# Attention's products in two 64-row groups on two banks, with a merged Gram product and a re-ordered list of work

## The chip, the cores and the metric

The kernel runs on one core of a Trainium2 chip. The metric is device time in microseconds (us), the median of three runs of one kernel: 1371.57 us for the kernel before, its runs from 1369.68 to 1371.94.

## What is computed

The reference is an attention over 32 pooled queries, a mixture of eight experts, and a gated product, one after the other. Batch, heads, sequence and head size are 8, 8, 576 and 64, so there are 4608 tokens of width 512.

```python
def _attn_ref(q, k, v, p):                      # p: 32 pooled queries per head
    p_packed = sm_attn(p, k, v)                 # softmax(p k^T / 8) v, 32 x 64 per head
    return sm_attn(q, p_packed, p_packed)       # softmax(q pp^T / 8) pp
def _moe_ref(x, expert_emb, tau, w1, w2):       # D=512, E=8, F=1024
    logits = xn @ en.T / tau                    # both normalised; one expert per token
    ...
        h = np.maximum(x[mask] @ w1[e], 0.0)
        out[mask] = gate_w[mask, None] * (h @ w2[e])
def _moe2_ref(x, w_a, w_b, w_out):              # d_ff = 1536
    return (x @ w_a * (x @ w_b)) @ w_out
```

## The kernel before

The kernel runs three stages, one after the other on TensorE: attention, experts (class `Moe`), gated product (class `Moe2`). A planner (`Sched`) decides the order of the work when the program is built. Each step is an `op` with the engines it may use, an assumed duration on each, the ops it depends on, a priority (lower goes first) and the buffers it takes and frees. `run` repeatedly takes, among the steps that could start earliest by the assumed durations, the one of lowest priority, and emits its instructions. Each engine, and the SP queue with its DMAs, then runs its own list strictly in that order.

**Attention, per batch.** `prep` loads p, k and v, transposes p and k on TensorE (`pT_mm`, `kT_mm`), and multiplies the pooled queries with the keys (`s1_mm`, lines 302 and 307). Heads come in pairs: a 128-row transposed tile holds two tokens' 64 rows, an even one above an odd one. `s1_mm` reads all 128 rows, with weights that are zero in the half not wanted (p is laid between zero columns in `pz`, and transposed in two positions `a`). So each group `g` of heads takes two products `a`, each into one bank of PSUM, with four heads in four 32-column groups of the array. `s1_ev` copies the scores to SBUF, `mx` and `exp` make the softmax there. `eT_mm` transposes the exponentials, and `pp_mm` (line 373) multiplies them with v: its two groups `g` lie in rows 0 to 63 and 64 to 127, in two banks. `ppT_mm` turns the result, `gr_mm` (lines 412, 413) makes for each head the 32 x 32 Gram matrix of the pooled values and its products with the eight expert embeddings, and `gr_ev` spreads the former into a block-diagonal matrix of 128 columns by multiplying with `blk`.

`query` loads and transposes q, and `rest` works in `NW` = 3 units of three token groups per batch. One unit is `s2_mm` (scores against the pooled keys, line 496, weights of 64 columns), `mx`, `sub`, `exp`, `total`, `norm`, a transpose `aT_mm`, and `x_mm` (line 539), which multiplies the attention weights with the 128 + 8 columns of the block-diagonal Gram matrix and the expert products, one product per token group and `g`, over all 128 rows. `dots`, `sq` and `add` make from it the eight dot products and the squared norm of each token in `c.nd`.

**PSUM** has eight banks. Attention uses three tags: `tr` (four banks: all transposes, `s1`, `gr`, and what the expert stage does ahead), `sm` (two: `s2` and `pp`) and `x` (two: `x_mm`).

**Experts.** `experts` chooses the expert for one batch of nine token groups: a product with `c.pair` (line 691), some 14 short steps on VectorE (recorded on line 672), one power on GpSimd (line 701). Batches 0 to 6 are done within attention and batch 7 at the start of the expert stage. `Moe.fetch` loads the weights of that expert, `zed` (line 961) multiplies the pooled keys with its first weights (512 columns at a time, four heads in four column groups, all 128 rows with zero halves, for each `g` into its own bank), and `up_mm` and `down_mm` follow. Batch 0's loads and its `zed` lie within attention, the other seven within the expert stage. `pT_dram` keeps the transposed pooled keys with their zero halves, 128 KB for each `g`.

Of the kernel before, what the change touches and what calls it, by code (L numbers as in the profile page):

```python
# [22 lines left out]
NI = NT // 64  # L23
AHEAD = 0.65
QA = 1.5
# [9 lines left out]
def make_consts(nc, c, keep, pool, emb, tau, psum, en, esq):  # L35
# [7 lines left out]
    c.blk = pool.tile([128, 4, NP], F32, name="blk")  # L43
    nc.gpsimd.memset(c.blk, 0.0)
    for j in range(4):
        nc.gpsimd.memset(c.blk[32 * j:32 * j + 32, j, :], 1.0)
# [25 lines left out]
class Sched:  # L72
# [4 lines left out]
    EPS, LAT, SAME = 0.05, 0.2, 0.06  # L77

# [11 lines left out]
    def op(self, engs, fn, deps=(), prio=0.0, take=(), free=(), lat=None, bias={}, start=0.0, after=None,  # L90
           behind=(), land=0.0):
# [6 lines left out]
        o.behind, o.land = behind, land  # L98
# [5 lines left out]
    def run(self, most=None, **clock):  # L104


        todo = list(self.ops)
        while todo:
            cand = []
            for n, o in enumerate(todo[:most]):  # L110
# [14 lines left out]
                for e, dur in o.engs.items():  # L125
                    at = max([clock.get(e, 0.0), ready.get(None, 0.0)]
                             + [d.end + (self.SAME if d.eng == e and d.lat <= self.LAT else d.lat) for d in o.deps])
                    key = at + dur + o.bias.get(e, 0.0)
                    if best is None or key < best[0]:
                        best = (key, at, dur, e)  # L130
# [6 lines left out]
            o.eng, o.end = e, at + dur  # L137
            if e != "none":
                clock[e] = o.end
# [10 lines left out]
NW = CI // 3  # L150


def attention(ctx, tc, c, q, k, v, p, a_dram, pT_dram, consts, more):
    nc = tc.nc
    W = 4 * NP + E
# [3 lines left out]
    for name, pools in dict(io="kvq", kt=["pT", "kt"] + [f"kT{m}" for m in range(4)], q=["qT"], e=["e", "eT"],  # L159
# [5 lines left out]
    ps_pool = dict(tr=c.ps_tr, sm=c.ps_sm, x=c.ps_x)  # L165
    pzs = [sb["pT"].tile([128, 2, 3 * D], F32, name=f"pz{i}") for i in range(2)]
    for t in pzs:
        nc.vector.memset(t, 0.0)
# [7 lines left out]
    own["a"] = [sb["a"].tile([128, 12, NP + 1], F32, name=f"as{i}") for i in range(sizes["a"])]  # L176
    for g in range(2):
        own[f"ppT{g}"] = [sb["pc"].tile([128, 4, 2, NP], F32, name=f"ppT{g}{i}") for i in range(sizes[f"ppT{g}"])]
# [5 lines left out]
    S_ = Sched(sizes)  # L184
    op, Buf = S_.op, Sched.Buf
# [11 lines left out]
    def psum(n, key):  # L197
        T_[key] = ps_pool[n].tile([128, 512], F32, tag=n, name=n)
        return T_[key]
# [11 lines left out]
    o_en = op({"T": 0.33}, en_mm, take=[t_en], prio=-4.0, start=EN0)  # L211
# [9 lines left out]
    def prep(b):  # L221
# [25 lines left out]
        def pT_mm(e):  # L247
            ps = psum("tr", ("pTp", b))
            tile_("pT", ("pT", b), [128, 2, 2, 128])
            for g in range(2):  # L250
                for a in range(2):
                    nc.tensor.transpose(
                        ps[:, (2 * g + a) * 128:(2 * g + a + 1) * 128], T_["pz", b][:, g, (1 - a) * D:(3 - a) * D],
                        c.ident)

        def pT_ev(e):
            copy(e, T_["pT", b], T_["pTp", b].rearrange("p (g a q) -> p g a q", g=2, a=2))

        t, bpT = Buf("tr"), Buf("pT")
        o = op({"T": 0.44}, pT_mm, deps=[o_p], prio=at(0), take=[t, bpT], free=[bp])  # L260
        o_pT = op({"A": 0.47, "V": 0.6}, pT_ev, deps=[o], prio=at(0), free=[t])
# [19 lines left out]
        for m in (0, 1, 2, 3, 4):  # L281
            t = Buf("tr")
            bkT.append(Buf(f"kT{m}" if m < 4 else "kt"))
            o = op({"T": 0.44}, kT_mm(m), deps=[o_k[m // 2]] if m < 4 else o_k, prio=at(0.05 * m), take=[t, bkT[m]],
# [5 lines left out]
        for g in range(2):  # L290
            def s1_mm(a, g=g):
                def f(e):
                    ps = psum("tr", ("s1p", b, g, a))
                    if (g, a) == (0, 0):
                        tile_("e", ("e", b), [128, CI, 2, D])

                    def w(j):
                        h = 2 * j + g
                        return T_["pT", b][:, h // 4, a, h % 4 * 32:h % 4 * 32 + 32]

                    for j in range(4):
# [3 lines left out]
                    if a == 0:  # L305
                        for j in range(4):
                            nc.tensor.matmul(
                                ps[32 * j:32 * j + 32, 256:320], lhsT=w(j),
                                rhs=T_["kT", b, 4][:, j, 64 * g:64 * g + 64], start=True, stop=True)
                return f  # L310

            def s1_ev(a, g=g):
                def f(e):
                    s = (slice(0, 5), slice(5, 9))[a]
                    n = s.stop - s.start
                    copy(e, T_["e", b][:, s, g], T_["s1p", b, g, a][:, 0:n * D].rearrange("p (i q) -> p i q", i=n))
                return f

            def mx(e, g=g):
                T_["mx", b, g] = m = st.tile([128, 1], F32, tag="mx1", name="mx1")  # L320
                nc.vector.tensor_reduce(out=m, in_=T_["e", b][:, :, g], axis=AX.XY, op=ALU.max)
                nc.vector.tensor_scalar(out=m, in0=m, scalar1=-0.125, scalar2=None, op0=ALU.mult)
# [1543 lines left out]
```

## Time and profile before

| | us |
|---|---|
| median of three runs | 1371.57 |
| the profiled execution, its own time | 1371.34 |
| its span, from the first to the last instruction | 1369.5 |
| TensorE busy | 1335.0 (97%) |
| VectorE busy | 790.8 (58%) |
| ScalarE busy | 591.9 (43%) |
| GpSimd busy | 106.5 (8%) |
| DMA | 278 MB, mean 203 GB/s |

PE is TensorE's products, PEld its loads of weights, DVE is VectorE, ACT ScalarE, POOL GpSimd, SPq the queue of SP, from which nearly all DMAs are issued. Busy time is the union of the durations, and a product's duration includes its way through the array: where products overlap, the time from the start of one group to the start of the next says more of its cost than its duration.

### The profile page before, as it was taken

To read this page: it belongs to the slowest core of one execution; us is meant where nothing else is said; L and a number is where in the kernel's file an instruction comes from. 1 tells how busy PE (TensorE), PEld (TensorE's weight loads), DVE (VectorE), ACT (ScalarE), POOL (GpSimd) and SP (SyncE) were. 2 spreads that over 40 slices of the span, in tenths; PEclk is the share of its full clock that TensorE was granted. 3 is DMA by queue.
4 is the path that set the end of the run, shared out by engine and by line. 5 is a ranking of instruction groups with operands and counts; after the bars stand their busy time and mean duration, and the time that the engine had idled before them with its cause. 6 is when DMAs were issued, how large, how long until landed. Compare 5 with 4: busy or idle time off the path is not lost. (4 is left out here: it accounts for less than half of the span.)

```text
span 1369.5 us, 26692 instructions
## 1 busy us (share of the span) xinstructions
PE 1335.0 (97%) x10263; PEld 1214.9 (89%) x10263; DVE 790.8 (58%) x1635; ACT 591.9 (43%) x1222; POOL 106.5 (8%) x234
## 2 busy tenths in 40 slices
PE   8998989999999999999999999999999999999997
PEld 6767778999999998999899999999999989999996
DVE  5787867666766655798554356434634363444342
ACT  5656524444444434565533244234433442343232
POOL 1121210101001000000100010001000010001001
PEclk9999999999999999999999999999999999999999
DMA  8878366778876735777865576557655665556552
GB/s 286 279 244 258 119 223 228 253 241 262 289 247 200 238 116 187 254 254 268 254 170 162 162 232 176 161 157 221 188 160 160 206 199 159 160 166 198 160 161 65
DMA packets 169272, 278.04 MB, mean 203 GB/s; under 512 B 16937, under 2 KB 68521, under 8 KB 169137
## 3 DMA queue, kind: packets, MB, share of 16 engines
q1 hardware_dynamic: 162704, 257.35, 60.9%
q0 software_dynamic: 6272, 18.88, 4.0%
q8 instruction: 84, 1.38, 0.4%
q14 instruction: 52, 0.42, 0.1%
q10 hardware_dynamic: 160, 0.02, 0.0%
HBM read 219.04 MB, written 57.15 MB: 202 GB/s over the span
## 5 line engine op out<-in xcount | busy, mean ns | idle before, releaser
L1443 DVE TENSOR_TENSOR s<-s,s 128x384 f32<-128x384 f32 x324 | 176.8, 556 | 340.8 <-ACT s L1579 338.4
L765 PE MATMUL pb<-xq,wq 128*128 128x384 f32 x504 | 170.2, 338 | 1.5 <-DVE s L1443 0.7
L765 PE MATMUL pa<-xq,wq 128*128 128x384 f32 x504 | 169.6, 337 | 1.6 <-DVE s L1443 1.6
L1692 PE MATMUL o<-oh,gh 128*128 128x512 f32 x432 | 170.3, 394 | 0.9 <-ACT osb L1712 0.9
L1693 PE MATMUL o<-ol,gh 128*128 128x512 f32 x432 | 170.4, 394 | 0.0
L1694 PE MATMUL o<-oh,gl 128*128 128x512 f32 x432 | 170.4, 394 | 0.0
L767 PE MATMUL pa<-xq,wq 128*128 128x384 f32 x504 | 170.3, 338 | 0.0
L767 PE MATMUL pb<-xq,wq 128*128 128x384 f32 x504 | 170.1, 337 | 0.0
L766 PE MATMUL pb<-xq,wq 128*128 128x384 f32 x504 | 170.0, 337 | 0.0
L766 PE MATMUL pa<-xq,wq 128*128 128x384 f32 x504 | 169.9, 337 | 0.0
L765 PE MATMUL dn<-hh,w2h 128*128 128x288 f32 x512 | 153.0, 299 | 0.0
L1579 ACT COPY s<-pa 128x384 f32<-128x384 f32 x180 | 86.5, 481 | 149.9 <-PE pa L767 149.8
L767 PE MATMUL dn<-hh,w2l 128*128 128x288 f32 x512 | 151.0, 295 | 0.0
L766 PE MATMUL dn<-hl,w2h 128*128 128x288 f32 x512 | 150.3, 294 | 0.0
L1579 ACT COPY s<-pb 128x384 f32<-128x384 f32 x180 | 86.5, 481 | 140.7 <-PE pb L767 140.6
L765 PEld LDWEIGHTS dn<-hh,w2h 128*128 128x128 f32 x512 | 96.1, 188 | 11.7 <-ACT w2h L994 5.9
L765 PEld LDWEIGHTS pb<-xq,wq 128*128 128x128 f32 x504 | 94.7, 188 | 11.8 <-DVE c L1443 1.6
L765 PEld LDWEIGHTS pa<-xq,wq 128*128 128x128 f32 x504 | 94.7, 188 | 10.0 <-DVE s L1443 2.2
L766 PEld LDWEIGHTS pb<-xq,wq 128*128 128x128 f32 x504 | 94.6, 188 | 8.4
L766 PEld LDWEIGHTS pa<-xq,wq 128*128 128x128 f32 x504 | 94.6, 188 | 7.5
L1694 PEld LDWEIGHTS o<-oh,gl 128*128 128x128 f32 x432 | 81.0, 187 | 18.8
L766 PEld LDWEIGHTS dn<-hl,w2h 128*128 128x128 f32 x512 | 96.8, 189 | 0.0
(192 smaller groups left out, 2436.1 us busy)
## 6 DMA issues: line engine op xcount, KB each, us to landing
wq<-ws SPq DMA_DIRECT2D x420, 256.0 KB, 2.8
ws<-wq SPq DMA_DIRECT2D x84, 256.0 KB, 3.7
raw<-in_moe_w_dram SPq DMA_DIRECT2D x36, 512.0 KB, 6.2
rawb<-in_moe_w_dram SPq DMA_DIRECT2D x28, 512.0 KB, 9.1
k<-in_k_dram SPq DMA_DIRECT2D x16, 576.0 KB, 5.4
v<-in_v_dram SPq DMA_DIRECT2D x16, 576.0 KB, 5.5
q<-in_q_dram SPq DMA_DIRECT2D x16, 576.0 KB, 5.1
xr<-x2T SPq DMA_DIRECT2D x20, 384.0 KB, 4.9
```

The lines of the kernel that those rows point to most:

```text
L765: nc.tensor.matmul(ps, lhsT=wh, rhs=xh, start=start, stop=False, **kw)
L766: nc.tensor.matmul(ps, lhsT=wh, rhs=xl, start=False, stop=False, **kw)
L767: nc.tensor.matmul(ps, lhsT=wl, rhs=xh, start=False, stop=stop, **kw)
L1443: VT = lambda out, a, b, o: V.tensor_tensor(out=out, in0=a, in1=b, op=o)
L1579: A.copy(out=T[n, key], in_=ps[n, names_bank[key]])
L1692: nc.tensor.matmul(a, lhsT=gh[:, h, s], rhs=wh, start=first, stop=False)
L1693: nc.tensor.matmul(a, lhsT=gh[:, h, s], rhs=wl, start=False, stop=False)
L1694: nc.tensor.matmul(a, lhsT=gl[:, h, s], rhs=wh, start=False, stop=last)
```

## The change

1. `s1_mm` reads 64 rows instead of 128. The two positions `a` lie in two row groups, each with its own bank, and are one step. p is loaded twice side by side in place of the zeros (two DMAs), and transposed in two blocks instead of four. `mx` and `exp` read the scores from PSUM; the copies `s1_ev` are gone. `mx` has a second reduction, `exp` a second activation.
2. `x_mm` works in two row groups `r` on two banks, with 64 + 8 columns each, so each token group takes four products in place of two. `sq` and `dots` read both banks; dot products come in two parts that are added by `pairs`.
3. `zed` reads 64 rows; both `g` are one step in two banks, in attention too. `pT_dram` keeps 64 KB per batch.
4. `gr_mm` makes one 128-column product over all four heads and keeps the diagonal blocks by `blk`, in place of four of 32 columns.
5. Units of four and five token groups (two per batch) in place of three of three. `s2_mm` pairs two token groups in each product; the last of the five stands alone.
6. PSUM: `tr` keeps four banks; the other four are `two`, two tiles of two banks, for `s1`, `pp`, `s2`, `x` and `zed`.
7. `experts` is called twice, for batches 0 to 3 within attention and for 4 to 7 at the start of the expert stage.
8. The planner gets other durations and adds a priority offset for each kind of step (`SHIFT`), a bias against VectorE where ScalarE can do a step (`VB`), and a least time of 4.3 us for each 127 products (`LF`, `CHUNK`).

```diff
-QA = 1.5
+QA = 2.0
+    VB, SHIFT, CHUNK, LF = 0.0, {}, 127, 0.0
...
+        if self.SHIFT:
+            o.prio += self.SHIFT.get(".".join([x for x in fn.__qualname__.split(".") if x != "<locals>"][-2:]), 0.0)
...
+            if self.LF and e == "T" and o.mm:
+                mm, left, x = o.mm, dur, at
+                while had + mm >= self.CHUNK:
+                    k = self.CHUNK - had
+                    part = left * k / mm
+                    x, left, mm, had = max(x + part, chunk + self.LF), left - part, mm - k, 0
+                    chunk = x
+                had += mm
+                o.end = x + left
...
-NW = CI // 3
+UNITS = ((0, 4), (4, 5))
+NW = len(UNITS)
...
-    sizes = dict(tr=4, sm=2, x=2, k=3, v=3, q=3, qT=4, e=2, eT=2, a=2, an=3, aT=2, sq=2, pz=2, pT=2, kt=1,
+    sizes = dict(tr=4, two=2, k=3, v=3, q=3, qT=6, e=2, eT=2, a=2, an=3, aT=2, sq=2, pz=2, pT=2, kt=1,
...
+    S_.LAT, S_.VB, S_.SHIFT, S_.LF = 0.22, 0.15, SHIFT, 4.3
...
-            turn_ = T_["pz", b] = pzs[b % 2]
-            nc.sync.dma_start(out=turn_[:, :, D:2 * D], in_=p[b].rearrange("(g j) p d -> (j p) g d", j=4))
+            t = tile_("pz", ("pz", b), [128, 2, 2, D])
+            for r in range(2):
+                nc.sync.dma_start(out=t[:, :, r], in_=p[b].rearrange("(g j) p d -> (j p) g d", j=4))
...
+                for j in range(4):
+                    for a in range(2):
                         nc.tensor.matmul(
-                            ps[32 * j:32 * j + 32, 0:256].rearrange("q (i p) -> q i p", i=4), lhsT=w(j),
-                            rhs=T_["kT", b, j][:, :, 64 * g:64 * g + 64], start=True, stop=True)
...
+                            ps[32 * j:32 * j + 32, a, 0:256].rearrange("q (i p) -> q i p", i=4), lhsT=w(j, a),
+                            rhs=T_["kT", b, j][D * a:D * a + D, :, 64 * g:64 * g + 64], start=True, stop=True)
...
+                nc.vector.tensor_reduce(out=m[:, 0:1], in_=ps[:, :, 0:256], axis=AX.XY, op=ALU.max)
+                nc.vector.tensor_reduce(out=m[:, 1:2], in_=ps[:, 0, 256:320], axis=AX.X, op=ALU.max)
...
+                w = T_["ppT", b, g][rows, g]
+                nc.tensor.matmul(ps[:, 0:128], lhsT=w.rearrange("p j k -> p (j k)"),
+                                 rhs=w.rearrange("p j k -> p (j k)"), start=True, stop=True)
                 for j in range(4):
-                    w = T_["ppT", b, g][rows, j, g, :]
-                    nc.tensor.matmul(ps[32 * j:32 * j + 32, 0:NP], lhsT=w, rhs=w, start=True, stop=True)
...
+            for i in range(n):
+                off = 64 * (first + i)
                 for g in range(2):
-                    off = 192 * w + 64 * i
-                    nc.tensor.matmul(ps[64 * g:64 * g + 64, i * W:i * W + W], lhsT=T_["aT", b][:, g, off:off + 64],
-                                     rhs=T_["gr", b, g], start=True, stop=True)
...
+                    for r in range(2):
+                        nc.tensor.matmul(xp()[64 * g:64 * g + 64, r, i],
+                                         lhsT=T_["aT", b][rows2[r], g, off:off + 64],
+                                         rhs=T_["gr", b, g][rows2[r], r], start=True, stop=True)
...
+            def mm(e, f=f, st=st):
+                st["ps"] = psum()
+                for j in range(4):
+                    for g in range(2):
+                        rows = slice(D * g, D * g + D)
+                        nc.tensor.matmul(st["ps"][32 * j:32 * j + 32, g, :], lhsT=self.pr[rows, j, :],
+                                         rhs=self.raw1[j][rows, f], start=True, stop=True)
...
+                e_ops, g_ops = experts(nc, c, tmp, 0, KNOWN, tr)
+                e = chain(S, e_ops, 4.5 * KNOWN + LG, of(0, KNOWN), step=0.05)
...
+                moe.before(S, lambda: c.ps_two.tile([128, 2, 512], F32, tag="two", name="two"), 18.0, e)
```

## Rows read from the trace of the kernel before

**Rows 1.** Busy time of each engine by stage: attention, experts, gated product.

```profile
0.00:182.80 182.80, 163.11 (x3410) 127.41 (x3410) 137.50 (x433) 107.83 (x252) 34.21 (x49) 0.99 0.68 224
182.80:522.80 340.00, 338.08 (x2534) 315.25 (x2533) 216.71 (x352) 143.75 (x235) 30.27 (x40) 0.99 0.71 231
522.80:1369.50 846.70, 833.82 (x4323) 772.20 (x4321) 436.54 (x850) 340.28 (x736) 41.98 (x145) 1.00 0.62 187
```

**Rows 2.** Stretches of attention: PE, PEld, DVE, ACT, POOL, PEclk, DMA share, GB/s.

```profile
0.00:10.00 10.00, 4.75 (x23) 4.36 (x24) 4.53 (x17) 3.46 (x6) 3.73 (x21) 1.00 0.71 240
...
120.00:140.00 20.00, 16.73 (x331) 13.32 (x319) 13.95 (x49) 11.62 (x29) 4.63 (x5) 1.00 0.72 233
140.00:170.00 30.00, 28.68 (x726) 22.70 (x722) 25.03 (x88) 15.04 (x38) 5.12 (x5) 1.00 0.30 100
170.00:182.80 12.80, 7.15 (x78) 5.63 (x77) 9.91 (x35) 5.28 (x11) 1.79 (x1) 0.81 0.07 27
```

**Rows 3.** TensorE's timeline around 77 and 80 us: start, duration, count.

```profile
76.71 0.64 PE L302 MATMUL tr<-kT,pT 128*32 128x256 f32 x8
77.16 0.29 PE L307 MATMUL tr<-kt,pT 128*32 128x64 f32 x8
77.39 0.92 PE L539 MATMUL x<-gr,aT 128*64 128x136 f32 x12
78.23 0.33 PE L398 MATMUL tr<-ident,pc 128*128 128x128 f32 x1
78.49 1.13 PE L496 MATMUL sm<-ppT,qT 128*64 128x64 f32 x32
79.55 0.33 PE L458 MATMUL tr<-ident,q 128*128 128x128 f32 x1
...
80.25 0.27 PE L412 MATMUL tr<-ppT 64*32 64x32 f32 x7
...
80.50 0.64 PE L302 MATMUL tr<-kT,pT 128*32 128x256 f32 x8
81.07 0.33 PE L458 MATMUL tr<-ident,q 128*128 128x128 f32 x1
```

**Rows 4.** TensorE's timeline in the expert stage, around `zed`.

```profile
213.64 1.92 PE L961 MATMUL up<-raw,pr 128*32 128x512 f32 x16
215.49 0.40 PE L765 MATMUL dn<-hh,w2h 128*128 128x288 f32 x1
```

**Rows 5.** TensorE alone, 0.24 us within `pp_mm`: products begun.

```profile
70.78:71.02 0.24, 0.24 (x32) 1.00 0.96 401
```

**Rows 6.** Products of `zed` (line 961) in the expert stage: PE, PEld busy.

```profile
182.80:522.80 340.00, 26.93 (x224) 5.84 (x224) 0.99 0.71 231
```

**Rows 7.** Groups of instructions by line: count, busy us, mean ns, idle before.

```profile
L203 ACT COPY e<-tr 128x320 f32<-128x320 f32 (+1 forms) x28 | 11.1, 399 | 6.1 <-PE tr L307 4.7 <-PE tr L302 0.7
...
L252 PE MATMUL tr<-ident,pz 128*128 128x128 f32 x32 | 5.5, 298 | 4.9 <-POOL en L54 4.5 <-DVE gr L205 0.3
...
L691 PE MATMUL tr<-nd,pair 128*128 128x81 f32 x14 | 2.9, 292 | 0.0
```

**Rows 8.** Choice of experts within attention: line 672 (VectorE busy), line 701 (GpSimd busy).

```profile
0.00:182.80 182.80, 19.88 (x98) 0.99 0.68 224
...
0.00:182.80 182.80, 12.56 (x7) 0.99 0.68 224
```

**Rows 9.** VectorE's `sub` of the unit whose `s2_mm` begins at 78.49.

```profile
80.33 0.55 DVE L506 TENSOR_TENSOR as<-sm,mx 128x384 f32<-128x384 f32 x1
```

**Rows 10.** TensorE's waits in attention: us in total, times, longest.

```profile
PE tr L525 <- DVE sm L672: 3.0, 1, 3.0
PE sm L373 <- issue: 1.8, 1, 1.8
```

**Rows 11.** DMA queues in attention: packets, MB, share.

```profile
q8 instruction: 27, 0.44, 1.0%
```

**Rows 12.** Load of p: issue time on SP, minimum, median, maximum ns.

```profile
L229 SPq DMA_DIRECT2D pz<-in_p_dram x8: 367/432/858, 1.3 to 88.3; - x8
```

More of the change, by code (lines that the diff above doesn't have):

```diff
@@ L164, in attention @@
     st = ctx.enter_context(tc.tile_pool(name="a_st", bufs=4, side="right"))
[L165 to L168, printed above, removed]
+    ps_pool = dict(tr=c.ps_tr, two=c.ps_two)
     own = {n: [sb[n].tile([128, 2, CI + 1, D], F32, name=f"{n}{i}") for i in range(sizes[n])] for n in "kq"}
@@ L330, in rs, with exp @@
+            def exp(e, g=g):
+                T_["sm", b, g] = sm = st.tile([128, 2], F32, tag="sm1", name="sm1")
+                for a, s in ((0, slice(0, 5)), (1, slice(5, 9))):
+                    n = s.stop - s.start
+                    nc.scalar.activation(
+                        out=T_["e", b][:, s, g], in_=T_["s1p", b, g][:, a, 0:n * D].rearrange("p (i q) -> p i q", i=n),
+                        func=AF.Exp, bias=T_["mx", b, g], scale=0.125, accum_out=sm[:, a:a + 1])
             def rs(e, g=g):
@@ L337, in prep @@
-            for a in range(2):
-                t = Buf("tr")
-                o = op({"T": 0.46}, s1_mm(a), deps=[o_pT] + o_kT, prio=f(0.25), take=[t] if g + a else [t, be],
-                       free=[bpT] + bkT[0:4] + ([] if a else bkT[4:]))
-                evs.append(op(evict(256 if a else 320), s1_ev(a), deps=[o], prio=f(0.25), free=[t]))
-            o = op({"V": 0.94}, mx, deps=evs, prio=f(0.33))
-            o = op({"A": 0.97}, exp, deps=[o], prio=f(0.37))
+            t = Buf("two")
@@ L366, in f @@
                 if i0 == 0:
-                    for g in range(2):
-                        psum("sm", ("ppp", b, g))
+                    psum("two", ("ppp", b))
                 for i in range(i0, i1):
@@ L509, in exp @@
+            T_["a", t] = T_["a1", t][:, :, 0:NP]
+            nc.vector.tensor_tensor(out=T_["a", t], in0=s3(), in1=wide(T_["mx2", t]), op=ALU.subtract)
         def exp(e):
@@ L552, in add @@
         def add(e):
-            nc.vector.tensor_reduce(out=c.nd[:, 3 * t:3 * t + 3, E], in_=T_["sq", t], axis=AX.X, op=ALU.add)
-        B_ = {n: Buf(n) for n in ("a", "an", "sq", "sm")}
-        f = lambda x: 1.5 * t + x
-        used = sorted({i // 2 for i, _ in runs})
-        o = op({"T": 0.6}, s2_mm, deps=[o_qT[x] for x in used] + ppT_ops[b, 0] + ppT_ops[b, 1], prio=f(0),
-               take=[B_["sm"]], free=[bqT[x] for x in used] + [T_["bppT", b, g] for g in range(2)])
-        o = op({"V": 0.55}, mx, deps=[o], prio=f(0))
@@ L569, in rest @@
-        x = Buf("x")
-        o = op({"T": 0.86}, x_mm, deps=[o_T, gr_ops[b, 0], gr_ops[b, 1]], prio=f(0.7), take=[x],
+            nc.vector.tensor_reduce(out=c.n2[:, nd], in_=T_["sq", t], axis=AX.X, op=ALU.add)
+        B_ = {m: Buf(m) for m in ("a", "an", "sq", "two")}
+        f = lambda x: 4.5 * b + 2.0 * w + x
+        used = sorted({i // 2 for i in tokens})
+        V = lambda m: 0.12 + 0.0011 * m
+        m = 128 * n
+        o = op({"T": 0.352 * n}, s2_mm, mm=16 * (n - n // 2), deps=[o_qT[x] for x in used] + ppT_ops[b, 0] + ppT_ops[b, 1], prio=f(0),
+               take=[B_["two"]], free=[bqT[x] for x in used] + [T_["bppT", b, g] for g in range(2)])
@@ L977, in split_a @@
+            for g in range(2):
+                self.o_z[b, g, h] = o
     def split_a(self, S, s, p):
```

364 lines of the change are left out of this document (183 added, 181 removed).

## The prediction, made before the kernel was changed

> **What bounds the kernel now.** I read the busy time by stage first, because the three stages follow one another on TensorE. In the expert stage TensorE is busy 338.1 of 340.0 us, in the gated product 833.8 of 846.7, and in attention 163.1 of 182.8, with VectorE at 137.5 and ScalarE at 107.8 [rows 1]. All three are TensorE's; the third the diff doesn't touch, so it should only start earlier. Next come the stretches of attention, for the 19.7 us in which TensorE is idle: 5.25 at the start, 3.3 between 120 and 140 us, 5.65 at the end, where the mean granted clock is 0.81, part at 1.2 and part at 2.4 GHz, and 5.5 spread out [rows 2]. The DMAs' share is high early and 0.30 or less from 140 us on, so DMA is no bound over the stage. Third, TensorE's timeline, for what one product costs from its start to the start of the next, since durations overlap.
>
> **What a product costs.** A "round" is one product on each tile of the array that the group uses; each written product appears as two in the trace. Two groups fix a line: `zed` takes 1.85 us for 16 products on four tiles, so four rounds of 512 columns [rows 4]; `x_mm` takes 0.84 for 12 on two tiles, six rounds of 136 [rows 3]. That gives 0.82 ns per column and round and 0.17 us once per group (the drain and the change of tiles). It returns what other rows measured: `s1_mm` with two rounds of 256 and two of 64 would be 0.69 (0.68 measured), with two of 256 alone 0.59 (0.57), `gr_mm` 0.24 (0.25) [rows 3]. Only `s2_mm` misses: 16 rounds in 1.06 us are 0.056 each where its columns would give 0.04. So with weights of 64 columns a round costs at least 0.056.
>
> **Do row groups run side by side?** That decides most of the sum. In `pp_mm`, whose two groups already lie in two row groups and two banks, 32 products of 64 columns begin in 0.24 us, 7.5 ns each [rows 5]. A round of 64 columns lasts 52 ns by the line above, so seven to eight tiles are in flight where the columns alone allow four. Row groups do overlap, for tiles of 64 rows x 32 columns; no row has 64 x 64 tiles, which `x_mm` will use. The Trainium skill (TensorE: Matmul & The Clock Gate, Part 1, "Wait — 56ns, not 53.3ns?") says that products never start closer than about 25 ns apart however few columns they have. The 7.5 ns in this trace contradict that between different tiles; by the rule the new `x_mm` would cost 72 x 25 ns per batch and the gain from it would be a third of what I take.
>
> **The terms, TensorE.**
> - `s1_mm`: 16 products over eight tiles and 8 over four are again two rounds of 256 and two of 64, 0.68, where 0.68 + 0.57 stood. 16 groups: -9.1. If row groups gave nothing it would be 1.11: -2.2.
> - `x_mm`: before 24 x 0.84 = 20.2. After, 32 and 40 products on four tiles are 8 and 10 rounds of 72 columns at 0.059, with two starts: 1.40 a batch, 11.2 in all: -9.0. If weights for the two row groups loaded one after the other, a round would cost 0.112: 2.36 a batch, -1.3. I take the first, because in `pp_mm` the weights of eight tiles keep up with 7.5 ns.
> - `s2_mm`: 16 + 24 rounds at 0.056 with two starts, 2.58 a batch for 3 x 1.06: -4.8. It keeps all 128 rows, so this comes from fewer products alone.
> - `zed`: two rounds of 512 per half in place of four, 0.84 less. Today the 224 products in the expert stage keep TensorE busy for 26.9 us [rows 6], and 14 halves give -11.8 there. Batch 0 in attention, four groups of 1.01 become two: -2.0. Without overlap: nothing, and -0.3.
> - p: half of the 32 transposes, which were busy 5.5 us [rows 7]: -2, not under -1.8, half being overlap.
> - `pairs`: seven products of 81 columns, 2.9 us in all [rows 7], become one of 288 columns twice and 36, by the line 1.2: -1.7. The second such product replaces one of 0.4 in the expert stage: +0.8.
> - `gr_mm`, the one that gets dearer: two products of 128 columns on one tile (0.38 with a start), then the small ones on other tiles (0.18), for 0.25: +0.31 by the line, +0.1 if the change of tiles hides. I take +0.25, 16 times: +4.0.
>
> Attention -9.1 - 9.0 - 4.8 - 2.0 - 2.0 - 1.7 + 4.0 = -24.6, leaving TensorE some 138 us busy; expert stage -11.8 + 0.8 = -11.0.
>
> **The other engines**, so that nothing replaces it. VectorE loses seven choices of experts, 19.9 us in attention, and gets one of four times the width, which I estimate at 5; 40 fewer unit steps save their fixed parts, two reductions of the scores from PSUM cost more. Near 120 us it stays under TensorE. ScalarE loses most of the copies of scores (28 of 32, 11.1 us [rows 7]) and has 16 more activations. GpSimd does one power on 36 columns for seven on nine, which cost 12.6 us [rows 8]; it was busy 34 of 182.8, and only batches 0 to 3's experts wait for it, whose weights are first needed by batch 0's `zed`. That moves later, with 4 MB of weight loads, into the stretch where DMA is at 0.30 and below [rows 2]. Those loads hide there as long as they land before the stage ends.
>
> **Waits.** All of `s1`, `pp`, `s2` and `x` now share two tiles of two banks. `s2` holds its bank from 78.49 to 80.88 [rows 3, 9], 2.4 us. With that as a scale I put the holds at 4.5 for each `s1` (until `exp` is done), 4.5 for `pp`, 3 and 4 for `s2`, 2 and 2.5 for `x`: 25 a batch, 12.5 for two tiles, against some 18 to 20 us that a batch takes. It fits, with less slack: behind a product that waits for a tile stands all of TensorE's list. At the end, TensorE's one wait of 3.0 us for VectorE, which was doing batch 6's choice of experts [rows 10], falls away; against it the last unit is five token groups long and not three. Also in attention is a wait of 1.8 us in the midst of `pp_mm` which the profile puts to no releaser [rows 10]; 27 transfers of instructions serve the stage's 6820 [rows 11], and the same number must now come in less time. The second DMA for p puts 0.43 us of SP's time ahead of the first keys [rows 12]. Of the idle time I take 2 us more than before: bounds -8 (the re-ordered list recovers the 3.3 and most of the spread, and the 3.0) and +12 (half a microsecond more ahead of each of the 16 `s2` and 8 `pp`).
>
> **The sum.** 1369.5 - 24.6 + 2.0 - 11.0 = 1335.9 us of span. The profiled execution took 1.84 us more than its span and lies 0.2 under the median, so its own time becomes 1337.7; I say 1337.5 against 1371.57. That is -2.5%, and 0.2% (2.7 us) is about what these runs can tell from no change.
>
> **The rivals.**
> - A: *two tiles are too few.* If an average hold is 6 us and not 3.6, seven holds on two tiles take 21 us a batch, as long as one takes now. Attention then gains about 4, the expert stage 11: 1356. For it speaks that in-order engines lengthen each hold, and that two units of `s2` and `x` got longer. Against it, the 2.4 us of the measured hold. The Trainium skill (TensorEngine Tiling, Restrictions and Gotchas, Gotcha 1) says that row tiles need different banks, which is why each product takes two.
> - B: *row groups don't overlap as used here*, so the change does little of what it says: -2.2 - 0.5 - 4.8 - 0.3 - 2 - 1.7 + 4 + 0.8 + 2 = -4.7, 1367. Rows 5 speak against it.
> - C: *a least distance between products with wide weights.* `s2_mm`'s 32 products in 1.06 us are 33 ns apart [rows 3], and if that holds for 64-column weights on any tile, `x_mm` takes 72 x 0.033 = 2.4 a batch (-1 in place of -9): 1345.5. Rows 5 speak against it, but with 32-column weights. The Trainium skill's rule weighed above is a mechanism of this kind.
> - D, on the other side: *instructions come too slowly.* As many products in less time, and bursts of 144 in `pp_mm`. If each of 27 transfers made TensorE wait as that one wait did, 1.8 us, the 27 waits would be 49 where one is paid now, and the kernel would take 1385. From 1.4 us each it is slower than before. One such wait in the trace of before speaks against it.
>
> **How the numbers follow.** My forecast, with its own range of 1327 to 1350: 0.80. A 0.09, B 0.04, C 0.03, D 0.04. The low end is the idle time's good bound (-10 from the sum), the high end both of idle's bad bound and `x_mm`'s poor one (+10 and +7.7), which takes in A: 1327 to 1357. Faster by over 0.2%: 0.80 + 0.09 + 0.03 and half of B, 0.94. Within 0.2%: the other half, 0.02. Slower: 0.04.
>
> **What would show it.** TensorE's first `up` product at 160 us and not at 182.8, the first `pa` product at about 489. `x_mm`'s products begin in fours, and 32 of them take about 0.64 us; `s1_mm` in eights, 24 in 0.68; a half of `zed` 1.0. The 14 halves of `zed` are busy about 15 us. The gated product is unchanged at 847. Wrong would be: products in pairs where I expect fours (B), TensorE waiting long and often for `exp`, `sub` or `sq` ahead of `s1`, `s2` and `x` (A), or waits without a releaser in attention of more than 5 us in all (D).

## The result, and the profile after

The changed kernel takes 1356.98 us (median of four runs, 1352.42 to 1360.91) against 1371.76 for the kernel before beside it: a ratio of 0.9893 with a 95% interval of 0.9859 to 0.9927. It is faster by 14.8 us where 34 were forecast. The profiled execution took 1357.94 us, 1.84 over its span of 1356.1.

The stages of the changed kernel, as in [rows 1]: length, PE, PEld, DVE, ACT, POOL busy, PEclk, DMA share, GB/s.

```profile
0.00:171.60 171.60, 144.38 (x3450) 117.30 (x3450) 118.99 (x291) 95.04 (x239) 24.84 (x35) 0.97 0.69 223
171.60:506.40 334.80, 327.59 (x2545) 314.51 (x2538) 222.35 (x354) 145.73 (x239) 34.60 (x40) 0.99 0.74 235
506.40:1356.10 849.70, 835.84 (x4322) 774.65 (x4320) 436.91 (x850) 339.90 (x736) 42.01 (x145) 1.00 0.62 187
```

Attention gained 11.2 us where 22.6 were forecast, the expert stage 5.2 where 11.0 were, and the gated product lost 3.0 where nothing was expected. The span shrank by 13.4 us. In attention TensorE's idle time is the length less the busy time: 27.2 us, against 19.7 before, and the granted clock is 0.97 on the mean, against 0.99.

TensorE's timeline in attention, clear of waits: the start of one group to the start of the next is its cost, as in [rows 3].

```profile
41.52 0.66 PE L328 MATMUL two<-kT,pT 64*32 64x256 f32 x16
41.98 0.31 PE L332 MATMUL two<-kt,pT 64*32 64x64 f32 x8
42.22 0.73 PE L570 MATMUL two<-gr,aT 64*64 64x72 f32 x32
...
45.97 1.15 PE L517 MATMUL two<-ppT,qT 128*64 128x64 f32 x32
...
48.95 0.86 PE L570 MATMUL two<-gr,aT 64*64 64x72 f32 x40
49.73 1.20 PE L376 MATMUL tr<-ident,e 128*128 128x128 f32 x9
```

`s1_mm` takes 0.70 us for its 24 products (41.52 to 42.22; forecast 0.68) and `x_mm` 0.78 for 40 (48.95 to 49.73; 0.76). In the expert stage `zed`'s 224 products keep TensorE busy for 14.1 us, where 15 were forecast and [rows 6] had 26.9:

```profile
L997 PE MATMUL up<-raw,pr 64*32 64x512 f32 x224 | 14.1, 597 | 0.3 <-DVE hl L1062 0.3
```

So these products cost what was forecast, and most of the loss is in what stands between them. TensorE's waits in attention (us in all, times, longest); "issue" means that the profile shows nothing that it waited for:

```profile
PE two L392 <- issue: 8.9, 6, 3.0
PE tr L279 <- DMA pz<-in_p_dram: 4.9, 1, 4.9
...
PE two L517 <- issue: 2.1, 2, 1.7
PE tr L376 <- ACT e L349: 2.0, 1, 2.0
...
PE tr L479 <- issue: 0.6, 1, 0.6
```

The waits without a releaser are 11.6 us in nine pieces; in the kernel before they were 2.7, of which [rows 10] has the largest. All other waits and small gaps together are 15.6 us, against 17.0. Counts of products are counts of the trace, where each written product shows as two. Where the waits sit is seen around 150 us (start, duration, count, idle time before):

```profile
144.41 1.59 PE L517 MATMUL two<-ppT,qT 128*64 128x64 f32 x48
145.93 0.32 PE L392 MATMUL two<-v,eT 64*32 64x64 f32 x10
147.93 0.77 PE L392 MATMUL two<-v,eT 64*32 64x64 f32 x54 [1.68 <-issue]
148.62 0.33 PE L376 MATMUL tr<-ident,e 128*128 128x128 f32 x1
148.89 0.97 PE L392 MATMUL two<-v,eT 64*32 64x64 f32 x73
151.93 0.31 PE L392 MATMUL two<-v,eT 64*32 64x64 f32 x7 [2.08 <-issue]
```

Both waits fall inside `pp_mm`, and between them lie 54 + 1 + 73 = 128 products. The second is followed by a lower clock (windows just before it ends and after it):

```profile
149.80:153.20 3.40, 0.86 (x15) 0.64 (x11) 0.90 (x3) 0.08 (x1) 0.00 (x0) 1.00 0.00 0
153.30:156.70 3.40, 3.40 (x45) 2.93 (x45) 0.92 (x3) 2.10 (x5) 0.00 (x0) 0.50 0.11 24
```

TensorE was busy for 0.86 of 3.40 us, and for the next 3.4 us, all busy, it had 1.2 GHz. From the end of the first wait to the end of the second are 4.0 us for the 128 products, and through the second wait the DMAs moved nothing (0 GB/s).

### The profile page after: what moved, and what is told of

It reads as the page before. It is cut to its first block, busy times and chain, and to the rows that moved or that the text cites. A ratio compares the mean times of both kernels' runs of the same rounds, so it can differ in the third digit from the quotient of the medians.

```text
span 1356.1 us, 26618 instructions
## 1 busy us (share of the span) xinstructions
PE 1307.8 (96%) x10307; PEld 1206.5 (89%) x10307; DVE 778.2 (57%) x1494; ACT 580.7 (43%) x1213; POOL 101.4 (7%) x220
## 4 chain that ended last, share of the span: by engine, by line
PE 88%; DMA 4%; DVE 3%; issue 2%; ACT 2%; POOL 1%; SPq 0%; ACTq 0%; POOLq 0%; DVEq 0%
PE o L1725 7%; PE o L1726 7%; PE o L1727 7%; PE pb L805 6%; PE pa L805 6%; PE pa L807 6%; PE pb L807 6%; PE pb L806 6%; PE pa L806 6%; PE dn L805 5%; PE dn L806 5%; PE dn L807 5%; PE up L805 2%; PE up L806 2%; PE up L807 2%; DMA out_dram<-osb 2%
## 5 line engine op out<-in xcount | busy, mean ns | idle before, releaser
L805 PE MATMUL dn<-hh,w2h 128*128 128x288 f32 x512 | 152.4, 298 | 0.0
L805 PEld LDWEIGHTS pa<-xq,wq 128*128 128x128 f32 x504 | 94.9, 188 | 11.4 <-DVE s L1476 3.7
L807 PEld LDWEIGHTS dn<-hh,w2l 128*128 128x128 f32 x512 | 96.4, 188 | 0.0
```

What stands on the lines that cost most here:

```text
L805: nc.tensor.matmul(ps, lhsT=wh, rhs=xh, start=start, stop=False, **kw)
L807: nc.tensor.matmul(ps, lhsT=wl, rhs=xh, start=False, stop=stop, **kw)
```

## The experiments

The theories. **S**, supply: TensorE's instructions arrive in pieces, and it waits where it has used up a piece before the next is there. **W**: two tiles of PSUM, or engines that are late with them, lengthen attention (the forecast's rival A). **E**: the choice of experts for four batches at once makes VectorE late at the start of the expert stage. Later ones are **B**, S with the waits only where bursts of products outrun the pieces, and **L**, batch 0's late work as the cause at the start of the expert stage.

| run | us | ratio to before | attention | PE busy | PEclk | waits without releaser |
|---|---|---|---|---|---|---|
| before (profiled) | 1371.34 | 1 | 182.8 | 163.1 | 0.99 | 2.7 |
| after (profiled) | 1357.94 | 0.9893 | 171.6 | 144.4 | 0.97 | 11.6 |
| 1024 products more, after | 1389.97 | 1.0121 | 208.9 | 171.9 | 0.86 | 23.3 |
| 1024 products more, before | 1418.88 | 1.0334 | 229.4 | 193.6 | 0.88 | 19.4 |
| thin pooled-key product | 1338.47 | 0.9746 | 152.4 | 132.9 | 0.99 | 2.0 |
| piece distance 0 | 1367.15 | 0.9958 | 186.7 | 154.7 | 0.90 | 10.3 |
| no offsets | 1360.17 | 0.9914 | 177.7 | 150.3 | 0.94 | 7.2 |
| piece distance 6.0 | 1371.64 | 0.9991 | 195.2 | 157.0 | 0.88 | 6.8 |
| lighter loads | 1352.56 | 0.9861 | 165.7 | 145.1 | 0.96 | 5.0 |
| 128 products fewer | 1358.99 | 0.9910 | 170.9 | 147.1 | 0.94 | 7.5 |
| 224 products fewer | 1360.33 | 0.9912 | 180.8 | 151.0 | 0.92 | 12.8 |
| wide pooled-key product | 1354.51 | 0.9873 | 165.9 | 145.2 | 1.00 | 1.6 |
| after, again | 1361.64 | 0.9917 | 177.2 | 148.7 | 0.94 | 12.8 |

Times are medians but for the two profiled ones, and the ratio is to the kernel before, measured beside each on the same chip; the chips differ between some of the runs. The other columns are from each run's profiled execution. "Products more" and "fewer" count as the trace does.

**How pieces arrive.** A kernel of its own: 512 small products (1024 in the trace) in one stretch while 16 MB load, 512 more with nothing else on the DMAs, and twelve long products around each.

```python
for i in range(n):
    for g in range(2):
        for j in range(4):
            r = slice(64 * g, 64 * g + 64)
            nc.tensor.matmul(ps[32 * j:32 * j + 32, g, 0:64], lhsT=x[r, 32 * j:32 * j + 32],
                             rhs=x[r, 64 * j:64 * j + 64], start=i == 0, stop=i == n - 1)
```

> This kernel computes nothing of the reference: it runs 512 small products (64 rows x 32 columns of weights, 64 columns, as in pp_mm; 1024 in the trace) between long ones, once with no other transfer under way and once beside 16 MB of loads, and stores one tile. Theory S (TensorE's instructions are delivered in pieces of about 127 products, and a piece takes 3.4 us or more to come): after the first pieces the small products go at 27 to 34 ns each, so 28 to 34 us for the 1024, in steps. Theory W (what holds attention back is waits for its two shared tiles of PSUM): 7 to 8 ns each throughout, 7 to 8 us. If loads delay the pieces, the second stretch takes clearly longer than the first.

The loads ran beside the first stretch. TensorE's timeline in this kernel, of the loaded and of the unloaded stretch:

```profile
16.29 2.16 PE L45 MATMUL ps<-x 64*32 64x64 f32 x199
23.11 2.04 PE L45 MATMUL ps<-x 64*32 64x64 f32 x128 [4.66 <-issue]
29.58 2.04 PE L45 MATMUL ps<-x 64*32 64x64 f32 x128 [4.43 <-issue]
36.05 2.04 PE L45 MATMUL ps<-x 64*32 64x64 f32 x128 [4.43 <-issue]
42.25 2.04 PE L45 MATMUL ps<-x 64*32 64x64 f32 x128 [4.16 <-issue]
48.17 2.04 PE L45 MATMUL ps<-x 64*32 64x64 f32 x128 [3.88 <-issue]
51.62 2.04 PE L45 MATMUL ps<-x 64*32 64x64 f32 x128 [1.42 <-issue]
...
75.81 2.04 PE L45 MATMUL ps<-x 64*32 64x64 f32 x128 [1.81 <-issue]
79.82 2.04 PE L45 MATMUL ps<-x 64*32 64x64 f32 x128 [1.96 <-issue]
83.55 2.04 PE L45 MATMUL ps<-x 64*32 64x64 f32 x128 [1.69 <-issue]
```

Its loaded stretch as a window (PE, PEld, DVE, POOL, PEclk, DMA share, GB/s), and the instruction queue of the whole run (packets, MB, share):

```profile
19.00:48.00 29.00, 8.16 (x512) 7.24 (x512) 0.00 (x0) 0.00 (x0) 0.54 0.98 365
```

```profile
q8 instruction: 16, 0.26, 0.7%
```

Instructions come in pieces of 128 products and as many loads of weights, about one transfer of the instruction queue for each (16 for the run's 2120 products). A piece is done in 2.04 us, with a granted clock of 0.54 over the stretch, and the next is then waited for. The first 199 products, and 175 in the second stretch, ran before the first wait. Beside full loads a piece comes every 5.9 to 6.5 us, without them every 3.7 to 4.0, and 3.5 just after the loads had ended. Of the 1024 products the loaded stretch took 39.8 us and the other 28.5, where W had said 7 to 8. Attention's 3450 products are 27 pieces in 171.6 us, 6.4 us each on the mean; the two waits shown above end 4.0 us apart, which is the distance seen here without loads.

**Is it the supply? More products, and fewer.** 1024 tiny products were added to `gr_mm` of either kernel, and `pp_mm` was cut to three of its nine token groups `i`.

```diff
+                for n in range(8):
+                    for j in range(4):
+                        nc.tensor.matmul(ps[32 * j:32 * j + 32, 140:141], lhsT=w[:, j], rhs=c.enT[rows, j, 0:1],
+                                         start=True, stop=True)
...
+                    if i % 4:
+                        continue
```

> The changed kernel with 64 further small products (128 in the trace) per batch within gr_mm, one column each, written beside what is read; the output stays the reference's. They cost TensorE 13 to 14 ns each by the pace of the old gr_mm, 14 us in all. S: eight more pieces of instructions at 3.4 to 4.3 us in a stage that already waits for them, so 25 to 34 us slower than the changed kernel, with waits without a releaser well above its 11.6 us. W: 14 us slower, those waits unchanged.

> The same 64 further products per batch in the kernel before, whose pieces are 6.3 us apart on average. S: its supply has slack, so 14 to 20 us slower than the kernel before, less than the changed kernel loses by the same addition. W: 14 us, as there.

> The changed kernel with pp_mm reduced to three of its nine token groups: 768 products fewer in the trace, six pieces of instructions less, nothing else taken from the list of work or its order. It leaves out two thirds of the pooled sums, and the count that decides on the fallback path is set to zero. Direct saving 768 x 6.7 ns, 5 us. S: the waits without a releaser fall from 11.6 to 4 us or less and the slow-clock stretches that follow them go, so 12 to 17 us faster than the changed kernel. W: 5 us faster, the waits stay.

The products cost 33 us in the changed kernel, as S said, and 46 in the one before, where S had expected 14 to 20: the slack that it had assumed was not there. In that run 11.1 of the 19.4 us of waits without a releaser stand in `gr_mm` itself, where the added products make bursts. The thinned kernel is 18.5 us faster, more than S's 12 to 17, hardly waits without a releaser (2.0 us), and has a clock of 0.99. W, which left the tiles of PSUM and the engines as the limit, expected much less in all three and is out as the main cause.

**The order of the list.** The planner's distance between pieces (`LF`, 4.3 us) set to 0 and to 6.0, and its offsets (`SHIFT`) emptied.

> The changed kernel with the planner's least time per 127 products set to 0, so that its order of work no longer counts with it. S: bursts of products stand closer together and the waits without a releaser grow beyond 11.6 us: 3 to 10 us slower than the changed kernel. W: within 3 us of it.

> The changed kernel with no priority offsets: the planner orders the same work by its plain priorities. If the re-ordered list is worth something, 5 to 20 us slower than the changed kernel; if the products alone make the gain, within 3 us.

> The changed kernel's list planned with a distance between pieces of 6.0 us in place of 4.3 (the smallest distance that was measured beside full loads was 6.2). Theory S: the list then spreads the bursts of products, waits without a releaser in attention fall from 11.6 us to about 6, and the kernel takes 1347 to 1355. If the order has no more to give, because the stage's products are as many and come no faster, 1355 to 1360.

Without the distance it is 10 us slower, the time that S named, but not by S's way: the waits without a releaser did not grow (10.3 us), and the rest is other waits and the clock (0.90). Without the offsets it is 3 us slower, little. A distance nearer to the measured one made it 15 us slower, against both expectations: the waits without a releaser fell to 6.8 us, but that list makes TensorE wait for VectorE instead (7.9 us at once for `an`), with the clock at 0.88. The planner can trade one wait for another; knowing the pieces better did not help.

**Is it the loads?** One ninth of each load of k and q from batch 2 on, the instructions unchanged.

```diff
-                out=turn("k", ("k", b, h))[:, :, 0:CI, :].rearrange("p m i d -> p m (i d)"), in_=halves(k, b, h))
+                out=turn("k", ("k", b, h))[:, :, 0:(CI if b < 2 else 1), :].rearrange("p m i d -> p m (i d)"),
+                in_=halves(k, b, h)[:, :, 0:(CI if b < 2 else 1) * D])
...
```

> The changed kernel, with one ninth of each load of k and q from batch 2 on (the rest of those buffers keeps the values of the batches before, and the flag of the dense path is held at zero): the same instructions in the same order, and some 12.5 of 28 MB of loads less. Theory S (instructions come in pieces of 128 products, and bulk loads on the same DMA engines slow the pieces): waits without a releaser in attention fall from 11.6 us to under 5, the slow-clock stretches inside attention go, the stage takes 160 to 164 us and not 171.6, the kernel 1345 to 1350. Rival W (tiles of PSUM and engines set the stage): the loads are ahead of their use anyway and nothing changes, 1355 to 1359.

```profile
PE two L393 <- issue: 4.1, 4, 1.8
...
PE two L519 <- issue: 0.9, 1, 0.9
```

In TensorE's waits in attention 5.0 us without a releaser are left of 11.6, nearly what S said. The stage became 5.9 us shorter, not 8 to 12, and the clock did not recover (0.96). Bulk loads do slow the pieces, here as in the small kernel; the two waits that stand around 150 us above stayed in part (0.7 and 1.8 us).

**Is it the number of products?** The list of work unchanged, the same columns in fewer products: in `s1_mm` one of 320 for one of 256 and one of 64 (128 fewer), then also one of 32 columns for the four small ones of `gr_mm` (224 fewer), and the same with a list planned anew.

```diff
+                        n = 5 - a
...
-                            ps[32 * j:32 * j + 32, a, 0:256].rearrange("q (i p) -> q i p", i=4), lhsT=w(j, a),
-                            rhs=T_["kT", b, j][D * a:D * a + D, :, 64 * g:64 * g + 64], start=True, stop=True)
...
+                            ps[32 * j:32 * j + 32, a, 0:64 * n].rearrange("q (i p) -> q i p", i=n), lhsT=w(j, a),
+                            rhs=T_["kT", b][D * a:D * a + D, j, 0:n, 64 * g:64 * g + 64], start=True, stop=True)
```

> The changed kernel, its list of work unchanged, with the keys of one batch in one tile, so that each product of 256 columns and the one of 64 beside it become one of 320: the same columns and rounds of work in s1, and 128 fewer products in attention (3322 for 3450), one piece of instructions. Theory S (in attention the number of products is the price, 24 ns each by the thinned pooled-key product, 32 ns each by the 1024 added): 3 to 4 us less, 1352 to 1355. Theory C (only columns and rounds cost): s1's 24 products took 0.70 us and the 16 take the same, the kernel 1356 to 1359.

> As the run before, and the four small products of gr with the experts' vectors become one of 32 columns, whose blocks one masked product on VectorE and a sum over two blocks pick out: 224 fewer products in attention in all (3226), the list of work unchanged. Theory S: 224 by 24 to 32 ns is 5.4 to 7.2 us less than the changed kernel, 1350 to 1353, and waits without a releaser under 9 us in attention. Theory C: gr's small products, 0.18 us a time, become 0.06, 16 times, 2 us, 1354 to 1357. In both VectorE takes over seven short copies from ScalarE, which costs nothing here.

> As the run before, with the smaller counts of products given to the planner, so that the list of work is made anew with the same distance between pieces. If the order of the list carries what the planner believes, 1346 to 1352; if a new order falls anywhere, as with a distance of 0 (10 us more) and of 6.0 (15 more), it lies between 1350 and 1368, and the run shows how far an order that was not tried on the chip can be trusted.

Waits without a releaser with 224 products fewer:

```profile
PE two L390 <- issue: 8.0, 4, 3.1
...
PE two L519 <- issue: 3.1, 1, 3.1
...
PE two L572 <- issue: 1.7, 1, 1.7
```

1358.99, 1360.33 and 1370.38: nothing was won. The 3 to 4 us of the first are no more than runs of one list differ by, but the second should have given 5.4 to 7.2, and S as a price for each product found no support. With 224 products fewer the pieces are 7.2 us apart on the mean, and yet TensorE waited 12.8 us for them, 8.0 of it in `pp_mm` (line 390 here). The list planned anew cost 10 us more, beyond both expectations, by other waits (10.3 us for `an`) and the clock (0.91).

**Is it the bursts?** `pp_mm` with weights of 64 columns and 128 columns of values: 36 products a batch for 72 (72 for 144 in the trace), at twice the columns, the list unchanged; and the changed kernel once more beside it.

```diff
-                        for j in range(4):
-                            nc.tensor.matmul(
-                                T_["ppp", b][32 * j:32 * j + 32, g, 0:D], lhsT=T_["eT", b][rows, i, 32 * j:32 * j + 32],
-                                rhs=T_["v", b, j // 2][rows, j % 2, i, :], start=(i == 0), stop=(i == CI - 1))
+                        for h in range(2):
+                            cols = slice(D * h, D * h + D)
+                            nc.tensor.matmul(
+                                T_["ppp", b][cols, g, 0:2 * D].rearrange("q (m d) -> q m d", m=2),
+                                lhsT=T_["eT", b][rows, i, cols], rhs=T_["v", b, h][rows, :, i, :],
+                                start=(i == 0), stop=(i == CI - 1))
```

> The changed kernel, its list of work unchanged, with the pooled-key products of two pairs of heads together: weights of 64 columns and 128 columns of values, of which each half of the rows keeps its own; 36 products for 72 a batch, 576 fewer of the 3450, all out of the bursts in which most waits without a releaser fall. By the cost line a batch has 18 rounds of 128 columns for 18 of 64: 0.94 us more, 7.5 in all; VectorE gets two short instructions more 16 times. Theory B (the waits fall where a burst runs ahead of the pieces): the 8.9 us of waits in the pooled-key products fall to under 2, with the slow clock after them, attention takes 166 to 171 us and the kernel 1351 to 1357. Rival (waits fall at the ends of pieces wherever these lie, 8 to 13 us in any list): the work is added in full, attention 177 to 182, the kernel 1361 to 1367.

> The changed kernel itself, on the same chip as the run before, to see what another execution of one list of work does with its waits and its clock. If both hang on the list alone, its waits without a releaser are 11.6 us again, at the same products, with three slow-clock stretches of 3.4 us in attention, and the times lie within 2 us of each other; if they hang on when pieces and loads arrive, waits and stretches differ and the times spread over 8 us, as the first four did (1352.4 to 1360.9).

Attention's window with wide products, and under it that of the changed kernel again:

```profile
0.00:165.90 165.90, 145.20 (x2875) 117.74 (x2875) 126.42 (x323) 95.07 (x239) 25.32 (x40) 1.00 0.71 231
```

```profile
0.00:177.20 177.20, 148.71 (x3450) 121.44 (x3450) 119.71 (x291) 95.70 (x240) 24.83 (x35) 0.94 0.68 219
```

Their waits without a releaser, in the same order:

```profile
PE two L399 <- issue: 1.0, 1, 1.0
...
PE two L528 <- issue: 0.6, 1, 0.6
```

```profile
PE two L392 <- issue: 11.3, 6, 3.0
...
PE tr L479 <- issue: 1.1, 1, 1.1
...
PE two L517 <- issue: 0.4, 1, 0.4
```

More columns and less time: 1354.51 against 1361.64 on the same chip. The waits fell from 12.8 to 1.6 us, TensorE's idle time from 28.5 to 20.7, and the clock stayed at 1.00 through attention. That is what B said. The run by itself does not part B from a price per product, since 576 products are gone as well: at 24 ns each (the thinned kernel's 18.5 us over its 768) they are 13.8 us, less 7.5 for the columns 6.3, about what was measured. What speaks for the bursts is that 224 products fewer elsewhere left 8.0 us of waits in `pp_mm`. A run with as many products and only the bursts spread was not made, so that the number counts for nothing is not shown. One list differs from execution to execution (1354.96 to 1367.38 in six runs, clock 0.97 and 0.94 in the two profiles); so differences of 2 or 3 us between single kernels here mean nothing.

**The expert stage.** `zed` alone in two row groups, in the kernel before; and the choice of experts in groups of (0 to 3), (4 to 6), (7), and of (0), (1 to 3), (4 to 7) with batch 0's work early.

```diff
-                    for g in gs:
-                        for j in range(4):
-                            nc.tensor.matmul(st["ps"][32 * j:32 * j + 32, g - gs[0], :], lhsT=self.pr[0][g][:, j, g, :],
-                                             rhs=self.raw1[j][:, f], start=True, stop=True)
+                    for j in range(4):
+                        for g in gs:
+                            rows = slice(D_ * g, D_ * g + D_)
+                            nc.tensor.matmul(st["ps"][32 * j:32 * j + 32, g - gs[0], :],
+                                             lhsT=self.pr[0][g][rows, j, g, :], rhs=self.raw1[j][rows, f],
+                                             start=True, stop=True)
```

```diff
+                for b0, b1 in ((0, 1), (1, KNOWN)):
+                    e_ops, g_ops = experts(nc, c, tmp, b0, b1, tr)
...
-                moe.before(S, lambda: c.ps_two.tile([128, 2, 512], F32, tag="two", name="two"), 18.0, e)
+                moe.before(S, lambda: c.ps_two.tile([128, 2, 512], F32, tag="two", name="two"), 14.0, speak[0])
```

> The kernel before with zed alone in two row groups on its two banks (the seven batches of the expert stage), in the order it had. The term of the forecast: 11.8 us faster than the kernel before. If the expert stage swallows the gain by itself: 5 us. Row groups without overlap: nothing.

> The changed kernel with the choice of experts for batches 0 to 3 and 4 to 6 in attention and batch 7 alone at the start of the expert stage, as before. Theory E (the fourfold choice of experts at the start of the expert stage makes TensorE wait 5 us more for VectorE there): 3 to 5 us faster than the changed kernel, its waits for hl back from 7 to about 2 us. Rival: those waits come from the splits of the weights and stay, so no gain, or 2 to 4 us slower for the steps moved into attention.

> The choice of experts for batch 0 alone again, early, its loads and its zed four units earlier; batches 1 to 3 together, 4 to 7 together as in the changed kernel. Theory L (what the expert stage fell short by, 5.7 us, is batch 0's late work: loads of its weights that land when the stage begins, and VectorE behind their halves): the 7.2 us that TensorE waits for hl at the start of the expert stage fall to under 3, the stage from up to pa takes 329 to 331 us and not 334.7, the kernel 1350 to 1354. Theory E2 (VectorE is late there because the wide choice of batches 4 to 7 stands in its list): the waits stay at 6 to 8 us and the time at 1356 to 1359. Either way one more choice costs attention up to 2 us.

`zed` alone gives 1361.30 (0.9914, 0.9896 to 0.9931): 11.6 us, the forecast's term of 11.8, with the expert stage at 328.8. The smaller choices (0.9998, 0.9983 to 1.0012) threw the whole gain away, beyond what their rival had said: TensorE waited 8.1 us at once for `hl` at the start of the stage, and 13.7 in all. E fell. Batch 0 early made the expert stage 331.5 us, and attention 178.1, in all 1360.89 (0.9924, 0.9907 to 0.9942). That looks like L, but the changed kernel run again had 331.9 with attention at 177.2, and with its work unchanged the stage took 330.4 us in the run with 128 products fewer and 335.6 in the one with wide products. So a difference of 3 us in one profiled execution says nothing, and L isn't shown.

**Both together.** Batch 0 early, and the merged `s1_mm`, each on top of the wide pooled-key product.

> The kernel with the wide pooled-key products, and batch 0's choice of experts alone and early, as tried before on the changed kernel (there the expert stage came to 331.5 us for 334.8, and attention lost 6.5). Theory B with L: with the bursts halved the new list costs attention under 3 us, its waits without a releaser stay under 3, the expert stage gains 3 to 5, and the kernel takes 1349 to 1354. If the earlier work costs attention by itself (VectorE and GpSimd late with an and pc), attention stays 5 us or more longer, and the kernel 1354 to 1360.

> The kernel with the wide pooled-key products, its list unchanged, and the keys of a batch in one tile, so that s1 has 16 products for 24: 704 fewer than the changed kernel in all. Theory B: waits without a releaser are 1.6 us already, so nothing is left to win, 1352 to 1356. If the number of products still has a price of its own (24 ns each), 3 us less, 1349 to 1352.

Batch 0 early costs: 1365.81 (0.9950, 0.9937 to 0.9963), attention 184.1 with only 2.1 us of waits without a releaser, but 9.5 for `an` and 5.9 for `pc`. That is slower than either expectation; whether its work in attention is the price, or the new list that comes with it, was not separated. The merged `s1_mm` gives 1352.61 (0.9859, 0.9837 to 0.9881), the same as the wide product alone (0.9873, 0.9858 to 0.9887), with 0.3 us of such waits and 165.7 us of attention for 165.9. No price on the number is seen; the 3 us that it would have been are about as much as these runs can tell.

## Why the prediction was wrong

**Right: what a product costs, and that row groups overlap.** Take from TensorE's busy time what the lower clock added, at most the missing share of the clock times the length: 144.4 - 0.03 x 171.6 = 139.2 us, where "some 138" were forecast, and 163.1 - 0.19 x 12.8 = 160.7 before, where the last stretch of [rows 2] alone was below full clock. By this estimate work fell by 21.5 us of 24.6. `zed`'s term stood when run alone. Rival B fell.

**The step that failed: "Of the idle time I take 2 us more than before."** Idle time rose by 7.5 us, 5.5 more than that, and all of it and more is waits without a releaser (8.9 us more). The clock took another 2.7 (0.03 x 171.6 = 5.1 us lost, against 2.4 before), which the sum had no term for. With the 3.1 of work that is, rounded, the 11.4 us missing in attention.

**Rival D was the mechanism in attention, under-weighted and mispriced.** It took the one wait of [rows 10] as the price of each of the 27 pieces [rows 11], 49 us in all, and then set its chance to 0.04 because there was only one. Pieces did not cost alike: nine waits fell on 27 pieces, and six of the nine, 8.9 of 11.6 us, in the bursts of `pp_mm`. The bursts of 144 in `pp_mm` were named there, and not followed up. Its mark, such waits of over 5 us in all, came true. Of A little is seen: the waits that can be for a tile (`zed` on `sq` 1.4 us, `s1_mm` on `pc` 0.8) are 2.2 us.

**Where the time fell is luck.** The 1356.98 us are nearly A's 1356, and lie at the very end of the stated 1327 to 1357. But A is not what happened: it had attention gain about 4 us and the expert stage 11, and 11.2 and 5.2 were measured. The bounds of the sum, +10 and +7.7, end at 1355; the 1357 were written to take in A. That the misses of three stages add up to A's price is chance.

**The 25 ns rule.** The Trainium skill (TensorE: Matmul & The Clock Gate, Part 1, "Wait — 56ns, not 53.3ns?") gives about 25 ns as the least distance from start to start. The prediction rejected that by the 7.5 ns of a burst, and for a burst over several tiles this holds: 40 products of `x_mm` took 0.78 us, 20 ns each. Over a long stretch in the small kernel 128 products every 3.7 us are 29 ns each, and 46 to 51 beside full loads, so as a mean the products are no closer than the rule says, from another cause.

**Expert stage and gated product.** The expert stage lacks 5.8 us. TensorE waits for `hl` in it for 7.2 us, 5.3 of them in its first 31 us, against 1.8 before:

```profile
PE up L805 <- DVE hl L1062: 5.9, 4, 2.5
PE up L732 <- DVE hl L1062: 1.0, 1, 1.0
...
PE up L997 <- DVE hl L1062: 0.3, 1, 0.3
```

VectorE stands there behind halves of batch 0's weights (`w2l`, until 177.0 us), which the change moved late: the forecast costed those loads at nothing "as long as they land before the stage ends", and what comes after them was left out. That this is the cause was not shown: bringing them forward moved the loss into attention, and the changed kernel run again had 5.1 us of these waits and a stage of 331.9. The 3 us of the gated product were not tested; a longer wait at its start (3.2 us on VectorE's `s`, 1.6 before) is part of them. So of the 20.2 us by which the span missed the forecast, the cause of 8.8 stays open.

## What to carry to other kernels

Where a stage is made of many small products, count them per microsecond as well as in columns: beside bulk loads this chip delivered a piece of 128 about every 6 us, and a burst that ran ahead of this waited, and after the longer waits was slowed by the clock. Look first at products that lie close together: fewer of them elsewhere won nothing here, and in the burst even twice the columns in half the products was faster. Work that is taken from the busiest engine of a stage with 10% idle time does not all come back, so give the idle time and the clock terms of their own, with the rival's mechanism as their upper bound.

## What the runs showed of the hardware that was not expected

- Pieces of 128 products, 3.5 to 4.0 us apart with idle DMAs and 5.9 to 6.5 beside 365 GB/s of loads; in attention eight of the nine waits fell at the same products of the list in both profiles of the changed kernel, with other lengths.
- After the waits of 3.0 and 2.1 us inside `pp_mm` (ending at 21.9 and 151.9 us) TensorE was at 1.2 GHz for some 3.4 us, and after the one of 1.7 us at 126 us it was not; at 81.6 us it fell to 1.2 GHz after three waits of 0.2 to 0.7 us. In the list planned with a distance of 6.0 the clock was 0.88 over 195.2 us, at most 23 us lost, partly after waits for VectorE.
- 64-row groups overlap for tiles of 64 x 64 (20 ns between products of 72 columns) and for 512 columns (`zed`, 14.1 for 26.9 us).
